# Attention and gated convolution: key sums moved between step 3's row work and `x`, groups of the last batch turned by DMA alone, and another order behind the last scores

## The chip, the cores and the metric

The kernel runs on one core of a Trainium2 chip. The metric is device time in microseconds (us). The measured kernel took 1134.94 us, the median of three runs that lay between 1133.9 and 1135.04 us. The engines are named as the profile names them: PE (TensorE matmuls), PEld (its weight loads), DVE (VectorE), ACT (ScalarE), POOL (GpSimd) and SP (SyncE, which here only issues DMAs). Each engine works off its own instructions strictly in program order.

## The reference, cut to what matters

```python
def _attn_ref(q, kv, w_sr):                 # q (4, 12288, 128), kv (4, 384, 32, 128)
    kv_pool = kv.reshape(B, H // r, r, W // r, r, C).mean(axis=(2, 4))     # r = 4
    k = v = kv_pool.reshape(B, -1, C) @ w_sr                               # 768 keys
    s = scale * (q @ k.transpose(0, 2, 1))
    a = np.exp(s - s.max(-1, keepdims=True))
    a /= a.sum(-1, keepdims=True) + 1e-09
    return a @ v

def _moe_ref(x, w_val, conv_w, w_out):      # x is the attention's output
    gate_pre[:, t] = sum(conv_w[k] * x[:, t - 4 + k] for k in range(5))    # causal, 5 taps
    return (sigmoid(gate_pre) * (x @ w_val)) @ w_out
```

All of it is float32. The last three weights reach the kernel as float64 words and are converted on the chip.

## The kernel before, in words

Channels lie on the partitions. There are 4 batches of 12288 queries and 768 keys. Queries are worked on in **groups** of 512, 24 to a batch, 96 in all; a group is four tiles of 128 queries, and the main loop (L470) makes one **step** for each tile, 384 steps, `gi` being the group and `j` (0 to 3) the step in it. The work of a step is written out by hand, and it belongs to several groups at once: scores are made one step ahead, and the groups that are 1, 2, 3 and 4 behind (`last`, `avg`, `xg`, `mg`) are in later stages.

What one tile goes through: three float32 products on PE give 128 x 768 scores `s` in PSUM (`score`, L250); DVE takes the negated row maximum `nm` (L256); ACT takes the exponential and its row sums `z` (L268). Each value is then split in two float16 halves, the high one by ACT (`p_hi`, L315), the low one by DVE one step later (`p_lo`, L319). The product with the values needs keys on the partitions, so tiles have to be turned. For tiles 0 to 2 (`NX = 3`), the halves go to a tile `hl` in SBUF, and a DMA transpose issued by SP writes them to `pt` (L323): one for tiles 0 and 1, issued behind the low half of tile 1, and one for tile 2, behind that of tile 2. Tile 3 is turned on PE instead (`turn`, L298): ACT writes the exponential to `pf`, six PE transposes of 128 x 128 put it back over the scores in PSUM, and the halves are written straight to `pt` (`pt<-s` in the profile).

Two groups later PE multiplies `pt` by the values, 18 products of 512 columns (`av`, L332), spread over the four steps as 7, 2, 3 and 6. Meanwhile DVE takes reciprocals of the row sums (`z`, L275, step 0), PE turns them (L278), DVE copies them out (`r`, L285, step 1), SP stores them (`rd`, L286) and reads them back to all partitions (`rb`, L291, step 3). In step 3 of the group that is two behind, DVE makes `x = av * down * rb` (L349), behind a 4-column copy by POOL (L345).

The second half of the network follows on `x`: taps and their sums on POOL (L359, L368; the fifth tap on ACT, L357), tanh on ACT (`th`, L384), the value product on PE in step 1 (`g_val`, L388, to `m`), `h` on DVE (L393), the output product on PE in step 2 (L398), a copy out on ACT (L408) and stores by SP in pairs of groups (L412). `m` is one PSUM bank, which the turned row sums, both products and the key setup use in turn.

Queries come in pairs of groups (L221) and are split in two on ACT (`qh`, L232) and POOL (`ql`, L236).

**Key setup.** A batch's keys come in 16 pieces of 384 KB (`load_kv`, L118, tile `kvt` with `AHEAD = 5` buffers). DVE sums each piece, 128 x 768 to 128 x 48 (`pool_kv`, L121), the whole is projected (L134), split (L143 to L147) and made into values. For batch 0 this is done ahead of the loop, and there every piece from the ninth on is followed by one operation of the weights' conversion (`convert`, 14 small DVE operations, L90 to L97); the other six are dripped in at two per step from step 6 on. For the next batch it is spread over the groups of the present one: `setup_steps` (L201) makes a list of which one entry is taken at the end of each group's step 3. An entry `piece(i)` issues the load of piece i + 2 (the first entry those of pieces 0, 1 and 2) and hands back the sum of piece i, which is executed in step 0 of the next group, behind `p_lo`. The entries for projecting and for the values follow. Small operations that a list `trickle` holds go out at two per step (`drip`).

```python
            return None, lambda: pool_kv(st, i)          # L208, executed at L513:
        if low and (j == 0 or t < NT):
            low()
```

Behind the loop (L536 on) the last groups, n1 (the last) to n5, are finished by a sequence written out by hand; there the gate of n2 and n1 is made on DVE (`conv_dve`, L374 and L376, tile `fast`), n1 in two halves of 256 columns.

## Time and profile before

| | us |
|---|---|
| median of the runs | 1134.94 |
| the profiled execution | 1133.22 |
| its span, first to last instruction | 1131.4 |
| PE busy | 1063.6 (94%) |
| DVE busy | 919.0 (81%) |
| ACT busy | 910.4 (80%) |
| POOL busy | 864.4 (76%) |
| key sums on DVE (L121), 64 of them | 60.5 |
| PE transposes of tile 3 (L298), 576 of them | 78.8 by modelled ends |
| time of the DMA packets of the SP queue, share of 16 engines | 85.4% |

The profile is of one execution. A busy share is a mean over the whole span. "Idle before" is the time an engine stood still ahead of an instruction, with what released it; the time at which one group follows another is read from an instruction that occurs once per group, here the reciprocal L275. Matmuls overlap and their ends are modelled, so on PE starts are compared, not durations. The mean granted clock of PE is 0.983 of full speed.

### The profile page before, as it was taken

The page shows a single profiled execution, that of the slowest core. Times are in us where ns is not written, and L with a number is a line of the kernel's source. Part 1 is how long each engine was busy: PE and PEld are TensorE (multiplying, and loading weights), DVE is VectorE, ACT ScalarE, POOL GpSimd, SP SyncE. Part 2 cuts the span into 40 slices and gives each one's busy share as a digit, 9 for nine tenths or more (in the row PEclk, how much of TensorE's full clock was granted, in tenths as well). Part 3 has the DMA queues.
Part 4 walks back from the last instruction along what each step waited for, and adds up shares of the span by engine and source line. Part 5 has one row for each costly group of instructions (what it writes and reads, how often), then busy time and mean ns, then how long its engine had stood idle before and what let it go on. Part 6 is the DMA issues. An engine that isn't in the chain of part 4 may idle for free.

```text
span 1131.4 us, 16595 instructions
## 1 busy us (share of the span) xinstructions
PE 1063.6 (94%) x5174; PEld 715.6 (63%) x5174; DVE 919.0 (81%) x1290; ACT 910.4 (80%) x1659; POOL 864.4 (76%) x948
## 2 busy tenths in 40 slices
PE   2879999999979999999997999999999999999996
PEld 1656666666756666666764666666666666666663
DVE  6868888888858888888885888888888888888884
ACT  1868888888858888888885888888888888888881
POOL 1168788878858888888885888887888888888872
PEclk9989999999989999999998999999999999999998
DMA  7779999887879999888876999898788888888872
GB/s 271 145 178 200 211 210 232 192 178 191 187 169 198 202 224 214 206 177 191 187 165 170 209 217 226 200 221 183 171 171 197 187 170 202 186 170 199 175 148 93
DMA packets 487095, 215.53 MB, mean 190 GB/s; under 512 B 453088, under 2 KB 453856, under 8 KB 487008
## 3 DMA queue, kind: packets, MB, share of 16 engines
q1 hardware_dynamic: 487008, 214.48, 85.4%
q8 instruction: 41, 0.67, 0.2%
q14 instruction: 46, 0.38, 0.1%
HBM read 75.83 MB, written 25.36 MB: 89 GB/s over the span
## 4 chain that ended last, share of the span: by engine, by line
PE 49%; DVE 25%; ACT 11%; issue 6%; POOL 5%; DMA 3%; SPq 1%; DVEq 0%; ACTq 0%
PE s L250 17%; PE av L332 16%; PE m L388 8%; DVE nm L256 8%; POOL ql L236 5%; ACT s L268 5%; DVE pool L121 4%; DVE pt L319 4%; ACT hl L315 4%; DVE x L349 4%; PE m L398 3%; PE s L298 3%; DMA kvt<-in_kv 3%; ACT qh L232 2%; DVE h L393 2%
## 5 line engine op out<-in xcount | busy, mean ns | idle before, releaser
L368 POOL TENSOR_TENSOR sum<-sum,tap 128x512 f32<-128x512 f32 x282 | 359.6, 1275 | 39.7 <-ACT tap L357 17.8
L332 PE MATMUL av<-pt,vh 128*128 128x512 f16 x1140 | 389.1, 383 | 0.0
L256 DVE TENSOR_REDUCE nm<-s 128x1 f32<-128x768 f32 x384 | 364.4, 949 | 3.7 <-PE s L250 3.7
L268 ACT ACTIVATE s<-s,nm 128x768 f32<-128x768 f32 x288 | 251.9, 875 | 125.5 <-DVE nm L256 124.3
L359 POOL TENSOR_SCALAR tap<-x,wm 128x512 f32<-128x512 f32 x376 | 253.4, 693 | 82.4 <-DVE x L349 80.9
L319 DVE SCALAR_TENSOR_TENSOR hl<-s,hl 128x768 f16<-128x768 f32 x288 | 273.1, 948 | 21.0 <-ACT hl L315 20.3
L250 PE MATMUL s<-kh,qh 128*128 128x384 f32 x768 | 253.3, 411 | 10.8 <-DVE hl L319 8.1
L315 ACT ACTIVATE hl<-s 128x768 f16<-128x768 f32 x288 | 233.3, 810 | 9.1
L332 PEld LDWEIGHTS <-vh 128*128 128x128 f16 x1164 | 114.0, 98 | 175.5 <-issue 85.8
L332 PE MATMUL av<-pt,vl 128*128 128x512 f16 x570 | 217.5, 382 | 0.0
L236 POOL TENSOR_TENSOR ql<-q,qh 128x512 fp32r<-128x512 f32 x96 | 121.8, 1269 | 122.6 <-ACT qh L232 122.6
L250 PE MATMUL s<-kh,ql 128*128 128x384 f32 x768 | 199.1, 341 | 0.0
L250 PE MATMUL s<-kl,qh 128*128 128x384 f32 x768 | 198.9, 340 | 0.0
L250 PEld LDWEIGHTS s<-kh,qh 128*128 128x128 f32 x768 | 132.4, 193 | 51.8 <-DVE hl L319 8.4
L349 DVE SCALAR_TENSOR_TENSOR x<-av,down,rb 128x512 f32<-128x512 f32 x95 | 71.4, 751 | 89.6 <-POOL ql L236 71.5
L250 PEld LDWEIGHTS s<-kl,qh 128*128 128x128 f32 x768 | 141.3, 190 | 0.5 <-DVE kl L147 0.5
L250 PEld LDWEIGHTS s<-kh,ql 128*128 128x128 f32 x768 | 140.9, 190 | 0.0
L388 PE MATMUL m<-x,wm 128*128 128x512 f32 x188 | 103.0, 630 | 25.0 <-DVE r L285 24.9
L368 POOL TENSOR_TENSOR sum<-tap,tap 128x512 f32<-128x512 f32 x94 | 120.4, 1281 | 0.0
L393 DVE SCALAR_TENSOR_TENSOR h<-th,m 128x512 f32<-128x512 f32 x94 | 64.7, 689 | 59.2 <-PE m L388 57.7
L315 ACT ACTIVATE pt<-s 128x768 f16<-128x768 f32 x96 | 77.8, 810 | 37.8 <-PE s L298 37.8
L332 PEld LDWEIGHTS <-vl 128*128 128x128 f16 x582 | 57.6, 99 | 77.9 <-issue 55.2
(68 smaller groups left out, 1068.9 us busy)
## 6 DMA issues: line engine op xcount, KB each, us to landing
kvt<-in_kv SPq DMA_DIRECT2D x64, 384.0 KB
rb<-rd SPq DMA_DIRECT2D x96, 256.0 KB
q<-in_q SPq DMA_DIRECT2D x47, 512.0 KB
out<-o SPq DMA_DIRECT2D x46, 512.0 KB
pt<-hl SPq DMA_TRANSPOSE x192
rd<-r SPq DMA_DIRECT2D x96, 2.0 KB
out<-o SPq DMA_DIRECT2D x3, 256.0 KB
q<-in_q SPq DMA_DIRECT2D x2, 256.0 KB
```

The source lines that it names most:

```text
L236: nc.gpsimd.tensor_tensor(out=g.ql, in0=g.q, in1=g.qh.bitcast(F32), op=ALU.subtract)
L250: nc.tensor.matmul(s[:, h, :HALF], a[:, sl], k[:, h * HALF:(h + 1) * HALF], start=(i == 0), stop=(i == 2))
L256: nc.vector.tensor_reduce(out=nm, in_=g.s[j], axis=AX.XY, op=ALU.max, negate=True)
L268: nc.scalar.activation(out=halves(g.pf[j]) if on_pe(j) else g.s[j], in_=g.s[j], func=AF.Exp, bias=g.nm.pop(j), accum_out=g.z[:, j:j + 1])
L315: nc.scalar.activation(out=part(g, j, 0), in_=g.s[j], func=AF.Copy, scale=2.0 ** 15)
L319: nc.vector.scalar_tensor_tensor(out=part(g, j, 1), in0=g.s.pop(j), scalar=2.0 ** 15, in1=part(g, j, 0), op0=ALU.mult, op1=ALU.subtract)
L332: nc.tensor.matmul(out, g.st[v][:, k * P:(k + 1) * P], g.pt[:, j0:j1, a * NCH + k], start=(i == 0), stop=(i == len(AV_ORDER) - 1))
L349: nc.vector.scalar_tensor_tensor(out=g.x[:, HALO + c0:HALO + c1], in0=av, scalar=g.st["down"], in1=g.rb[:, c0:c1], op0=ALU.mult, op1=ALU.mult)
L359: eng.tensor_scalar(out=g.tap[k], in0=src, scalar1=w, scalar2=1.0, op0=ALU.mult, op1=ALU.mult)
L368: nc.gpsimd.tensor_tensor(out=s, in0=acc, in1=g.tap[k], op=ALU.add)
L388: nc.tensor.matmul(m, wval, g.x[:, HALO + c0:HALO + c1], start=True, stop=True)
L393: nc.vector.scalar_tensor_tensor(out=h, in0=th, scalar=1.0, in1=m, op0=ALU.add, op1=ALU.mult)
```

## The change

- `NX` is replaced by a number of each group, `by_dma`: 4 for groups 0, 2, 4 ... 22 of the last batch, 3 for all others. With 4, no tile of the group is turned on PE: tile 3's halves go to `hl` (whose buffers grow from three tiles to four for all groups), and the DMA transposes are one for tiles 0 and 1 and one for tiles 2 and 3, the latter behind the low half of tile 3, so in step 0 of the next group.
- The sum of a piece is no longer handed back. The next entry of the list queues it in `pooling`, and it is executed in step 3 of the group after that, between `p_lo` and `x`. The list gets one entry more.
- The conversion of the weights leaves the prologue. All 14 operations go into `trickle` at step 3.
- The calls behind the loop are put in another order, with n1's two halves apart.

The diff:

```diff
@@ -17,7 +17,6 @@
 P = 128
 GQ = 512
 NT = GQ // P
-NX = 3
 
 
 class Group:
@@ -192,6 +191,7 @@
         return high, low
 
     trickle = []
+    pooling = []
 
     def value_steps(st):
         return [lambda: trickle.extend(column_scale(st)), lambda: None, lambda: None,
@@ -202,12 +202,13 @@
         def piece(i):
             if i == 0:
                 key_tiles(st)
+            else:
+                pooling.append(lambda: pool_kv(st, i - 1))
             for k in range(3) if i == 0 else (i + 2,):
                 if k < PIECES:
                     load_kv(b, st, k)
-            return None, lambda: pool_kv(st, i)
-
-        steps = [lambda i=i: piece(i) for i in range(PIECES)]
+
+        steps = [lambda i=i: piece(i) for i in range(PIECES + 1)]
         steps += [lambda h=h: project(st, h, misc()) or split_keys(st, h) for h in range(2)]
         return steps + value_steps(st)
 
@@ -256,16 +257,16 @@
         nc.vector.tensor_reduce(out=nm, in_=g.s[j], axis=AX.XY, op=ALU.max, negate=True)
         g.nm[j] = nm
 
-    def on_pe(j):
-
-        return j >= NX
+    def on_pe(g, j):
+
+        return j >= g.by_dma
 
     def expo(g, j):
         if j == 0:
             g.z = zs[g.i % len(zs)]
-        if on_pe(j):
+        if on_pe(g, j):
             g.pf[j] = pfp.tile([P, NK], F32, name="pf")
-        nc.scalar.activation(out=halves(g.pf[j]) if on_pe(j) else g.s[j], in_=g.s[j],
+        nc.scalar.activation(out=halves(g.pf[j]) if on_pe(g, j) else g.s[j], in_=g.s[j],
                              func=AF.Exp, bias=g.nm.pop(j), accum_out=g.z[:, j:j + 1])
 
     def norm_eps(g):
@@ -305,10 +306,10 @@
 
     def part(g, j, a):
 
-        if on_pe(j):
+        if on_pe(g, j):
             return pt_tile(g)[:, j, a * NCH:(a + 1) * NCH].rearrange("p (h k) q -> p h (k q)", h=2)
         if g.hl is None:
-            g.hl = hlp.tile([P, NX, 2, NK], F16, name="hl")
+            g.hl = hlp.tile([P, NT, 2, NK], F16, name="hl")
         return halves(g.hl[:, j, a])
 
     def p_hi(g, j):
@@ -318,8 +319,8 @@
 
         nc.vector.scalar_tensor_tensor(out=part(g, j, 1), in0=g.s.pop(j), scalar=2.0 ** 15,
                                        in1=part(g, j, 0), op0=ALU.mult, op1=ALU.subtract)
-        if j in (1, 2):
-            j0 = 0 if j == 1 else j
+        if (j % 2 or j == g.by_dma - 1) and not on_pe(g, j):
+            j0 = j // 2 * 2
             nc.sync.dma_start_transpose(
                 out=pt_tile(g)[:, j0:j + 1].rearrange("p j k q -> p (j k) q"),
                 in_=g.hl[:, j0:j + 1].rearrange("p j a k -> p (j a k)"))
@@ -421,6 +422,7 @@
         for i in range(NG):
             g = Group()
             g.i, g.b, g.t0, g.st = len(groups), b, i * GQ, states[b]
+            g.by_dma = 4 if b == B - 1 and i % 2 == 0 else 3
             g.s, g.nm, g.pf, g.hl, g.pt = {}, {}, {}, None, None
             groups.append(g)
     G = len(groups)
@@ -444,8 +446,6 @@
         if i == 3:
             convert = load_moe()
         pool_kv(st, i)
-        if i >= 8 and convert:
-            convert.pop(0)()
         if i == 3 * PIECES // 4:
             low()
         if i % (PIECES // 2) == PIECES // 2 - 1:
@@ -475,7 +475,7 @@
             load_pair(at(gi + 4), at(gi + 5))
         if gi % NG == 1 and j == 0 and at(gi + NG - 1):
             steps += setup_steps(cur.b + 1, states[cur.b + 1])
-        if t == NT + 2:
+        if t == 3:
             trickle += convert
 
         if nxt:
@@ -492,8 +492,9 @@
             high = None
         row_max(cur, j)
         expo(cur, j)
-        if on_pe(j):
+        if on_pe(cur, j):
             turn(cur, j)
+        if j == NT - 1:
             norm_eps(cur)
             if mg:
                 out_tile(mg)
@@ -513,6 +514,8 @@
         if low and (j == 0 or t < NT):
             low()
             low = None
+        if pooling and j == NT - 1:
+            pooling.pop(0)()
         if last and j == 0:
             norm_turn(last, misc())
         drip()
@@ -541,51 +544,51 @@
         return bank_pair()[:, 0]
 
     norm_reciprocal(n1)
-    p_lo(n1, NT - 1)
-    store_pair(n5)
+    av_part(n2, 0)
     norm_turn(n1, misc())
     n4.th = g_tanh(n4.gate)
-    norm_store(n1)
-    n4.m = g_val(n4, misc())
-    av_part(n2, 0)
-    norm_rows(n1)
     tap(n3, TAPS - 1, nc.scalar)
     g_conv(n3)
-    h = g_h(n4.th, n4.m)
+    p_lo(n1, NT - 1)
+    norm_store(n1)
+    store_pair(n5)
     for i in (1, 2, 3):
         av_part(n2, i)
+    norm_rows(n1)
+    n4.m = g_val(n4, misc())
     new_x(n2, n3, nc.scalar.copy)
     g_x(n2, n2.av)
-    n4.m = g_out(h, misc())
+    h4 = g_h(n4.th, n4.m)
     n2.m = g_val(n2, bank())
+    n4.m = g_out(h4, misc())
     out_tile(n4)
     g_evac(n4, n4.m)
     store(n4)
+    avs = [bank()[:, :half] for _ in cuts]
+    for i, av in enumerate(avs):
+        av_range(n1, av, 0, len(AV_ORDER), i * NT // 2, (i + 1) * NT // 2)
     n2.th = g_tanh(conv_dve(n2))
     new_x(n1, n2, nc.scalar.copy)
-    avs = [bank()[:, :half] for _ in cuts]
-    av_range(n1, avs[0], 0, len(AV_ORDER), 0, NT // 2)
-    h = g_h(n2.th, n2.m)
-    av_range(n1, avs[1], 0, len(AV_ORDER), NT // 2, NT)
+    g_x(n1, avs[0], *cuts[0])
+    h2 = g_h(n2.th, n2.m)
+    n2.m = g_out(h2, bank())
+    n1.th = work.tile([C, GQ], F32, name="th")
+    ths = [g_tanh(conv_dve(n1, *cuts[0]), n1.th[:, :half])]
     n3.m = g_val(n3, misc())
-    n2.m = g_out(h, bank())
-    ths = []
-    n1.th = work.tile([C, GQ], F32, name="th")
-    for av, c in zip(avs, cuts):
-        g_x(n1, av, *c)
-        ths.append(g_tanh(conv_dve(n1, *c), n1.th[:, c[0]:c[1]]))
+    n3.th = g_tanh(n3.gate)
     out_tile(n2)
     g_evac(n2, n2.m)
     store(n2)
-    n3.th = g_tanh(n3.gate)
-    h = g_h(n3.th, n3.m)
-    ms = [g_val(n1, bank()[:, :half], *c) for c in cuts]
-    hs = [g_h(th, m) for th, m in zip(ths, ms)]
-    n3.m = g_out(h, misc())
+    g_x(n1, avs[1], *cuts[1])
+    h3 = g_h(n3.th, n3.m)
+    ms = [g_val(n1, bank()[:, :half], *cuts[0])]
+    n3.m = g_out(h3, misc())
+    ths.append(g_tanh(conv_dve(n1, *cuts[1]), n1.th[:, half:]))
     g_evac(n3, n3.m)
     store(n3)
-    for h, c in zip(hs, cuts):
-        g_evac(n1, g_out(h, bank()[:, :half]), *c)
+    ms.append(g_val(n1, bank()[:, :half], *cuts[1]))
+    for th, m, c in zip(ths, ms, cuts):
+        g_evac(n1, g_out(g_h(th, m), bank()[:, :half]), *c)
         store(n1, *c)
```

## The prediction

> **What bounds the kernel now.** I read the page's busy shares first (PE 94%, so waits are few and local), then the reciprocal L275, which occurs once per group, by windows, for the pace of each stage. Columns: window, its length, DVE busy with these instructions (count), granted PE clock, DMA share, GB/s.
>
> ```profile
> 57.70:75.05 17.35, 0.17 (x1) 0.80 0.71 167
> 75.05:241.30 166.25, 2.51 (x15) 1.00 0.94 208
> 319.05:339.15 20.10, 0.17 (x1) 0.83 0.82 195
> ...
> 593.77:614.91 21.14, 0.17 (x1) 0.76 0.79 193
> 614.91:781.17 166.26, 2.51 (x15) 1.00 0.92 204
> 890.75:997.10 106.35, 1.68 (x10) 1.00 0.86 186
> ```
>
> Three paces stand there. Groups that sum keys take 166.25/15 = 11.08 us, 45 of them (the middle batch's 15 are the line left out). Groups of the last batch, which sum none, take 106.35/10 = 10.63. And one group in each of the first three batches takes 17.35, 20.10 or 21.14, at a lowered clock.
>
> What sets the two steady paces: the chain of waits in a key group (start, length, what), then DVE's and PE's timelines in a last-batch group (start, length, engine and line, in brackets the idle before).
>
> ```profile
> 419.47 0.28 DVE r L285
> 419.75 0.04 issue
> 419.79 1.14 PE m L388 x2
> ```
>
> ```profile
> 974.39 0.75 DVE L349 SCALAR_TENSOR_TENSOR x<-av,down,rb 128x512 f32<-128x512 f32 x1 [0.87 <-POOL ql L236]
> ...
> 977.72 0.27 DVE L285 COPY r<-m 4x128 f32<-4x128 f32 x1
> ...
> 985.00 0.75 DVE L349 SCALAR_TENSOR_TENSOR x<-av,down,rb 128x512 f32<-128x512 f32 x1 [0.87 <-POOL ql L236]
> ```
>
> ```profile
> 973.91 0.38 PE L332 MATMUL av<-pt,vh 128*128 128x512 f16 x1
> ...
> 978.53 1.02 PE L388 MATMUL m<-x,wm 128*128 128x512 f32 x2
> ...
> 989.15 1.02 PE L388 MATMUL m<-x,wm 128*128 128x512 f32 x2
> ```
>
> PE's value product (L388) writes the bank that `r` is copied from, so it can't start before `r` has ended. In the key group it starts 0.04 behind `r`: PE waits there, and a ring is closed, of x, row maximum, low half, key sum, row maximum, `r` (all DVE), value product and PE's work up to the last `av`, which the next x needs. In the last-batch group `r` ends at 977.99 and the product starts at 978.53, so the ring has 0.5 of slack and PE alone sets 989.15 - 978.53 = 10.62. The ring without a key sum is: product to x, 985.00 - 978.53 = 6.47 (x is released by the last `av`, which ends at 973.91 + 0.38 = 974.29, x starting at 974.39; the bracket's `ql` ends at the same time); x to the end of `r`, 977.99 - 974.39 = 3.60; and 0.04. Together 10.11. With a sum of 0.87 (row below) it is 10.98, and 11.08 was measured; 0.1 I can't place.
>
> The long groups have another cause, on DVE:
>
> ```profile
> 64.92 0.95 DVE L121 TENSOR_REDUCE pool<-kvt 128x48 f32<-128x768 f32 x1 [6.07 <-DMA kvt<-in_kv]
> ```
>
> The first piece's sum stands in DVE's queue one step after its load's issue; the row work behind it, and then PE, wait 6 us.
>
> **The change part by part.**
>
> *First sums.* A first sum now comes in step 3 of the second group behind its load, some 20 us after the issue, where the wait shown was 6.07. The wait goes, and what is late next is PE's own 10.62: 17.35 + 20.10 + 21.14 - 3 x 10.62 = **26.7**. The three loads issued together still put 1.1 MB ahead of the transposes and `rb`; I take nothing for it, and at most 1.5 in each of three groups.
>
> *The other sums.* In step 3 DVE stands idle 0.87 ahead of x (rows 974.39 and 985.00), and a sum takes 0.87 from start to start (row 22.58 below). It fits with nothing to spare, but even a later x doesn't count until the ring's 10.11 has grown by 0.5. So it costs nothing there and leaves the ring: 45 x (11.08 - 10.62) = **20.7**. If the cover were gone, each group would pay 0.87 less 0.5, some 17 of the 20.7. A buffer is free one group before the next load that takes it, so SP isn't held.
>
> Beside x there is a neighbour that step 0 didn't have, POOL's `ql`. Whether a sum on DVE is held by it, the prologue shows:
>
> ```profile
> 10.48 1.26 POOL L236 TENSOR_TENSOR ql<-q,qh 128x512 fp32r<-128x512 f32 x1 [9.18 <-ACT qh L232]
> ```
>
> ```profile
> 10.92 3.88 DVE L121 TENSOR_REDUCE pool<-kvt 128x48 f32<-128x768 f32 x4 [0.87 <-DMA kvt<-in_kv]
> ```
>
> Four sums, 0.97 each, start in the middle of a `ql` that ends at 11.74; neither is longer than elsewhere. I take nothing for it; a full hold is a rival below. The Trainium skill, page "SBUF — State Buffer", section "Who interferes with whom", has a rule that speaks against such neighbours: DVE and GpSimd share a port pair as an exclusive lock, and the loser blocks for the other's whole instruction. The same section exempts `tensor_reduce` on trn2, and the trace agrees: 0.97 beside a `ql`. By the lock alone the sum would come out as in that rival.
>
> *Last batch, even groups.* Their six PE transposes go, by the chain:
>
> ```profile
> 974.29 0.66 PE s L298 x6
> ```
>
> PE then needs 10.62 - 0.66 = 9.96, but the ring needs 10.11, and both meet at the value product, where PE waits in order and can't save up the rest. Saved: 0.51 x 12 = **6.1**; between 0 (something else sets these groups) and 12 x 0.66 = 7.9. ACT and DVE do the same work at other addresses. On SP's queue:
>
> ```profile
> 971.55 5.14 SPq L323 DMA_TRANSPOSE pt<-hl  x2
> ```
>
> Three tiles take 5.14, so two about 3.4. The second transpose now waits for the low half of tile 3, which DVE ends one row maximum ahead of `r`, near 976.9. It stands behind this step's `rb` and ahead of a store and of `rd`: issue to 980.3, `rd` about 2 later than now, which no one needs before the `rb` behind the next transposes; those come at 971.55 + 10.6 = 982.2. An estimate for its landing from the same row: 976.9 + 3.4 and half as much again, 982. The `av` that needs it begins about 1 behind the x of 985.00. Four microseconds are left, at a DMA share of 0.86 that rises by a third of the transposes in every second group.
>
> *Conversion.* The prologue's chain, and SP's issues of the last seven loads:
>
> ```profile
> 10.07 5.41 DMA kvt<-in_kv
> ...
> 16.46 0.20 DVE rest L90
> ...
> 22.58 0.87 DVE pool L121
> ```
>
> ```profile
> 10.07 7.80 SPq L118 DMA_DIRECT2D kvt<-in_kv  x7
> ```
>
> Seven conversions of 0.20 or somewhat more lie between the last sums; without them DVE could be done about 1.6 earlier. But the last load is issued near 17.5, and one took 5.41 to land, which is 22.9: the last sum (22.58) can hardly start earlier. I take **0.1**, between 0 and 1.6. In steps 4 and 5, where the pipeline fills and DVE is on the path, four operations of 0.20 come in; steps 6 to 8 had theirs before. I take **-0.6**, between 0 and -1.5.
>
> *Behind the last scores.* DVE's and ACT's rows, SP's `rb` for n2, and what an `rb` took to land in the chain:
>
> ```profile
> 1110.58 0.75 DVE L349 SCALAR_TENSOR_TENSOR x<-av,down,rb 128x512 f32<-128x512 f32 x1 [4.88 <-PE av L332]
> 1111.44 0.49 DVE L374 TENSOR_SCALAR fast<-x,wm 128x512 f32<-128x512 f32 x1
> 1111.96 3.11 DVE L376 SCALAR_TENSOR_TENSOR fast<-x,wm,fast 128x512 f32<-128x512 f32 x4
> ...
> 1117.35 2.05 DVE L376 SCALAR_TENSOR_TENSOR fast<-x,wm,fast 128x256 f32<-128x256 f32 x4
> ```
>
> ```profile
> 1128.33 0.38 ACT L408 ACTIVATE o<-s 128x256 f32<-128x256 f32 x1 [0.49 <-PE s L398]
> ```
>
> ```profile
> 1104.17 0.83 SPq L291 DMA_DIRECT2D rb<-rd  x1
> ```
>
> ```profile
> 74.83 2.89 DMA rb<-rd
> ```
>
> Now n2's `av` waits for a value product that waits for n1's `r`. Put first, its 18 products, for which DVE now waits 4.88, are done by about 1106. But n2's `rb`, issued at 1104.17 behind n1's transposes, lands 2.9 to 4 later, so x starts near 1108 instead of 1110.58. From there DVE sets the end: x 0.7, h of n4 0.6, gate 0.5 + 3.1, tanh 0.7, h 0.6, half a gate 2.4, half an x 0.5, h of n3 0.6, half a gate 2.4, tanh 0.5, half an h 0.4, half a product on PE about 1, copy 0.4: 14.4, to 1122.4, where it was 1128.71. That is 6.3. PE will idle for x once more, and a lowered clock (0.76 to 0.83 in the windows of the long groups) would hold up its 36 half products for n1. I take **5.0**, between 2 and 8.
>
> Sum: 26.7 + 20.7 + 6.1 + 0.1 - 0.6 + 5.0 = 58.0. The profiled execution took 1133.22, 1.8 more than its span of 1131.4 (the table above), and would take 1075.2; the median of the runs lies 1.72 above it: 1134.94 - 58.0 = **1076.9**.
>
> **The rivals.**
>
> *DMA takes over in the key groups.* For it: 0.94 at 11.08 is 10.4 of packet time a group, 0.98 at 10.62, and transposes and `rb` share one queue. Against it: in the whole span PE waited for a transpose 0.2 us:
>
> ```profile
> L332 PEld LDWEIGHTS <-vh 128*128 128x128 f16 x1164 | 114.0, 98 | 175.5 <-issue 85.8 <-DMA pt<-hl 0.2
> ```
>
> If these groups stay at 11.08, 20.7 is lost: 1097.6; half of that gives 1087.
>
> *The sum is held by `ql`.* Then it starts when `ql` ends, x slips by 0.87, the ring takes 10.98, and key groups stay at 11.0: 1094 to 1098. For it speaks the bracket at x, against it only the prologue's rows, in other surroundings.
>
> *The even groups give nothing.* The ring's unplaced 0.1 may be larger there, or ACT's work too tight: 1083.
>
> *Slower than before: the even groups' second transpose lands late.* It decides where it lands over 4 us later than I estimate. PE then stands at `av` in order, with all scores behind it. Groups in which the engines waited 6 us cost 6.7 to 10.5 each (windows above), clock included; twelve at 8.6 make 103, less the 51.9 of the other parts: 1186. It takes a two-tile transpose of over 8 us, where three tiles are issued in 5.14. The Trainium skill, page "TensorE: Matmul & The Clock Gate", Part 1, says that an idle window of about 3.4 us halves PE's clock; the windows' 0.76 to 0.83 agree.
>
> **How the numbers follow.** Forecast 0.80, DMA 0.07, `ql` 0.04, even groups nothing 0.07, late transpose 0.02. The low end takes all of 7.9, 8 behind the last scores and 1.6 in the prologue: 1076.9 - 6.3, rounded to 1070. The high end takes 2 behind the last scores (+3), the bursts (+4.5), and half of the DMA rival (+10): 1094. Outside are the full rivals near 1097 and the late transpose, 0.13 at most. About 0.2% is what a measurement of this kernel can tell from no change. Only the late transpose ends above it: faster 0.97, slower 0.02, and 0.01 for parts that cancel.
>
> **What would show it.** L275 should follow itself at 10.62 in key groups; in the loop no L121 should wait for its load and no interval exceed 12 us; in the last batch intervals near 10.1 and 10.6 should take turns. n2's x should start 17 to 18 before the span's end. The forecast is wrong if key groups stay above 10.8, if x starts more than 0.2 behind the last `av`, or if PE waits for `pt`.

## The result and the profile after

The changed kernel takes 1077.99 us, median of runs from 1075.04 to 1078.68; the kernel before, measured beside it, 1134.42 (1132.55 to 1135.04). The ratio is 0.950, 95% interval 0.9478 to 0.9522. The forecast was 1076.9. The profiled execution took 1078.68 with a span of 1076.9, which is 54.5 less than the span before; all of the following is about these 54.5.

First the reciprocal, now L276, by windows for the same stages as before (window, length, DVE busy with it, granted clock, DMA share, GB/s):

```profile
59.88:68.93 9.05, 0.17 (x2) 1.00 1.00 235
68.93:228.47 159.54, 2.50 (x15) 1.00 1.00 220
305.50:316.82 11.32, 0.17 (x1) 1.00 0.94 221
...
563.93:575.26 11.33, 0.17 (x2) 1.00 0.96 220
575.26:734.43 159.17, 2.50 (x16) 1.00 1.00 223
810.76:1051.02 240.26, 3.84 (x24) 1.00 0.98 202
1051.02:1076.91 25.89, 0.16 (x1) 0.91 0.42 116
```

Groups that sum keys follow each other at 159.54/15 = 10.64, 159.17/15 = 10.61 (11.08 before). The three long groups are 9.05, 11.32 and 11.33, at full clock (17.27, 20.09 and 21.13 before, from reciprocal to reciprocal; the prediction's windows read up to 0.08 more). The DMA share has risen from 0.94 to 1.00, and between the third and the last reciprocal neither PE nor DVE waits for a transfer. Where the 54.5 came from, as differences of these intervals between the two profiled executions:

| part | forecast | measured |
|---|---|---|
| first sums (three long groups, and the values groups that move into them) | 26.7 | 28.2 |
| the other 45 sums | 20.7 | 20.6 |
| last batch, even groups | 6.1 | 3.7 |
| up to the third reciprocal (conversion) | -0.5 | -2.1 |
| behind the last reciprocal | 5.0 | 4.1 |
| sum | 58.0 | 54.5 |

The setup list is one entry longer, so one 11.3 us group that makes values moves from the stretch ahead into the place of each long group; that is why two of these read 11.32 and not 10.62, and 0.70 has gone from each of the stretches ahead. The first row counts both. Likewise two such groups now stand at the start of the last batch: as a stretch it takes 240.26 against 242.48, and the third row has the 1.4 that moved into it taken out.

The key sum beside x, in DVE's and POOL's timelines of a key group:

```profile
408.98 0.96 DVE L320 SCALAR_TENSOR_TENSOR hl<-s,hl 128x768 f16<-128x768 f32 x1 [0.23 <-ACT hl L316]
409.86 0.94 DVE L120 TENSOR_REDUCE pool<-kvt 128x48 f32<-128x768 f32 x1
410.81 0.75 DVE L350 SCALAR_TENSOR_TENSOR x<-av,down,rb 128x512 f32<-128x512 f32 x1
```

```profile
409.54 1.27 POOL L237 TENSOR_TENSOR ql<-q,qh 128x512 fp32r<-128x512 f32 x1 [0.40 <-ACT qh L233]
```

The sum fills exactly the 0.87 in which DVE stood idle, and runs its usual 0.94 wholly beside `ql` (409.54 to 410.81); so do all 48 sums of the loop. The chain of waits in such a group consists of PE alone:

```profile
327.50 1.53 PE av L333 x7
329.03 0.11 PE m L279
329.14 1.07 PE s L251 x6
330.21 0.86 PE m L389 x2
```

No work of another engine stands in it. Over the whole span the profile's page gives this chain by engine, where before it gave PE 49% and DVE 25%:

```profile
PE 89%; DVE 5%; ACT 2%; DMA 2%; issue 1%; POOL 0%; SPq 0%; DVEq 0%; ACTq 0%
```

From 40 us on none of the 48 sums found DVE waiting for a load.

### The profile page after: what moved, and what is told of

It is laid out like the page before. It is cut to its first block, busy times and chain, and to the rows that moved or that the text cites. A ratio compares the mean times of both kernels' runs of the same rounds, so it can differ in the third digit from the quotient of the medians.

```text
span 1076.9 us, 16475 instructions
## 1 busy us (share of the span) xinstructions
PE 1038.4 (96%) x5102; PEld 706.5 (66%) x5102; DVE 919.5 (85%) x1290; ACT 903.7 (84%) x1659; POOL 865.2 (80%) x948
## 4 chain that ended last, share of the span: by engine, by line
PE 89%; DVE 5%; ACT 2%; DMA 2%; issue 1%; POOL 0%; SPq 0%; DVEq 0%; ACTq 0%
PE s L251 36%; PE av L333 32%; PE m L389 7%; PE m L399 7%; PE s L299 5%; DMA kvt<-in_kv 2%; DVE nm L257 1%; PE m L279 1%; ACT s L269 1%; ACT hl L316 1%; DVE hl L320 1%; DVE pt L320 1%; DVE pool L120 0%; DVE x L350 0%; PE m L176 0%
## 5 line engine op out<-in xcount | busy, mean ns | idle before, releaser
L369 POOL TENSOR_TENSOR sum<-sum,tap 128x512 f32<-128x512 f32 x282 | 360.3, 1278 | 22.1
L269 ACT ACTIVATE s<-s,nm 128x768 f32<-128x768 f32 x300 | 262.0, 873 | 88.7 <-DVE nm L257 80.0
L320 DVE SCALAR_TENSOR_TENSOR hl<-s,hl 128x768 f16<-128x768 f32 x300 | 284.8, 949 | 21.4 <-ACT hl L316 21.1
L316 ACT ACTIVATE hl<-s 128x768 f16<-128x768 f32 x300 | 243.0, 810 | 9.1
L399 PE MATMUL m<-h,wm 128*128 128x512 f32 x188 | 96.8, 597 | 1.2 <-DVE h L394 1.2
L389 PE MATMUL m<-x,wm 128*128 128x512 f32 x188 | 96.1, 592 | 0.0
```

Of the source, the lines that this page charges most:

```text
L269: nc.scalar.activation(out=halves(g.pf[j]) if on_pe(g, j) else g.s[j], in_=g.s[j], func=AF.Exp, bias=g.nm.pop(j), accum_out=g.z[:, j:j + 1])
L316: nc.scalar.activation(out=part(g, j, 0), in_=g.s[j], func=AF.Copy, scale=2.0 ** 15)
L320: nc.vector.scalar_tensor_tensor(out=part(g, j, 1), in0=g.s.pop(j), scalar=2.0 ** 15, in1=part(g, j, 0), op0=ALU.mult, op1=ALU.subtract)
L369: nc.gpsimd.tensor_tensor(out=s, in0=acc, in1=g.tap[k], op=ALU.add)
L389: nc.tensor.matmul(m, wval, g.x[:, HALO + c0:HALO + c1], start=True, stop=True)
L399: nc.tensor.matmul(m, wout, h, start=True, stop=True)
```

## The experiments

### The key sums: which step, how late, how much more

`late_step0` keeps the sum two groups behind its load but puts it back in step 0; `x_first` keeps step 3 but puts it behind x.

```diff
-        if pooling and j == NT - 1:
+        if pooling and j == 0:               # late_step0
```
```diff
-        if pooling and j == NT - 1:          # x_first: these two lines
-            pooling.pop(0)()                 # go behind new_x and g_x
```

> The changed kernel with the late sums put back into step 0 (one group later than in the kernel before, behind the low half of tile 3). Theory, the ring: a sum that lies between x and the copy of r is part of the ring x, r, value product, last av. The waits for the first loads stay away, but key groups go back from 10.62 to 11.08 us each: 48 x 0.46 = 22 us more than the changed kernel, about 1099. Rival, lateness: what helped the 45 other groups too was that the sum no longer comes close behind its load; then step 0 is as good as step 3 and the time stays near 1078.

> The changed kernel with the sum in the same step 3, but behind x instead of ahead of it. Theory, the ring: the sum now lies between x and r, so key groups take about 11.0 to 11.1 again, 1097 to 1100, although step, load and neighbours are the same. Rival, the balance of steps: the gain came from taking the sum out of step 0, where DVE has the reciprocal and the low half as well; then the order within step 3 makes no difference and the time stays near 1078.

Measured: 1100.12 (ratio 0.9704, 0.9687 to 0.972) and 1100.14 (0.9704, 0.9687 to 0.9722). By windows of the reciprocal in `late_step0`:

```profile
311.69:323.01 11.32, 0.17 (x1) 1.00 0.93 221
323.01:488.87 165.86, 2.51 (x15) 1.00 0.97 214
```

And in its chain, the ring is back, `r` and then the product:

```profile
402.76 0.28 DVE r L286
...
403.09 1.14 PE m L389 x2
```

The long groups are cured in both kernels (11.32), so it is the lateness that removes 26.7 or more; the key groups are at 165.86/15 = 11.06 in one and 166.55/15 = 11.10 in the other, so it is the place ahead of x that gives the 20.7. One instruction further, behind x, the sum is in a ring again and the whole gain of this part is gone. So the two gains can be told apart. In `x_first` it is not `r` that PE waits for: its products start 0.16 behind `r` and not 0.05, and the scores ahead of them 0.06 behind the end of tile 3's low half. That second way is taken up below, with the even groups.

`early_step3` lets each entry queue its own piece, so that the sum comes one group behind its load, ahead of x:

```diff
-            else:
-                pooling.append(lambda: pool_kv(st, i - 1))
             ...
+            pooling.append(lambda: pool_kv(st, i))
-        steps = [lambda i=i: piece(i) for i in range(PIECES + 1)]
+        steps = [lambda i=i: piece(i) for i in range(PIECES)]
```

> The changed kernel with the sum in step 3 beside x, but one group behind its load instead of two (an entry of the list queues the sum of its own piece). Theory, the ring: key groups stay at 10.62; the first sum of a batch comes one period (10.6 us) after the issue of three loads, which took about 9 us to land in the kernel before, so it waits between 0 and 2 us in three groups: 1078 to 1084. Rival, lateness: the 20 us of the key groups came from the later sum, and are given back: about 1098.

Measured: 1077.21 (0.9506, 0.9487 to 0.9525), equal to the changed kernel; by windows:

```profile
305.74:316.35 10.61, 0.17 (x1) 1.00 1.03 268
316.35:475.55 159.20, 2.51 (x15) 1.00 0.99 219
```

In the loop one sum of 48 waited for its load, 0.2 us, and one x waited 0.9 for its `rb` (an interval of 11.48, followed by 10.23). So step 3 of the next group is late enough, or nearly: the medians don't tell the two apart. The "about 9 us" of the expectation was too much; in the kernel before, the three loads land within 7.2 to 8.0 us of the first one's issue.

`extra_full` puts a second sum of the same size, whose output nothing uses, ahead of each real one in step 3:

```diff
-                pooling.append(lambda: pool_kv(st, i - 1))
+                pooling.append(lambda: more(st, i - 1) or pool_kv(st, i - 1))
```

> The changed kernel with each sum of the loop made twice (the first time into a tile that nobody reads), both ahead of x in step 3. Theory, the ring: the idle time ahead of x (0.87) holds one sum; a second one moves x by 0.87, of which the ring has 0.5 to spare in a group that PE sets at 10.62, by the r way, or 0.3 if the score bank's way (10.29 in the even groups of the last batch) is the longer one. So key groups take 11.0 to 11.2 and the time is 1095 to 1104. Rival, DVE is not near a limit there and x is not on a ring: the second sum goes into other idle time of DVE (h waits 0.8 for PE in each group) and the time stays below 1083.

Measured: 1092.98 (0.9645, 0.9625 to 0.9665). The key groups take 10.98 (window), and x now starts behind the second sum (DVE's timeline):

```profile
321.26:486.01 164.75, 2.52 (x15) 1.00 0.98 216
```

```profile
406.75 0.94 DVE L127 TENSOR_REDUCE pool<-kvt 128x48 f32<-128x768 f32 x1
407.61 0.74 DVE L357 SCALAR_TENSOR_TENSOR x<-av,down,rb 128x512 f32<-128x512 f32 x1
```

So the first sum is free and the second costs 0.36 of its 0.87: the rest is slack between x and PE. The size is that of the prediction's slack of 0.5, and the time, 1092.98, lies below my 1095 to 1104. But the slack that is used up is not the one over `r`. PE in the same group:

```profile
409.91 0.27 PE L286 MATMUL m<-ident,z 128*128 128x128 f32 x1
410.20 0.61 PE L258 MATMUL s<-kh,qh 128*128 128x384 f32 x2
```

The scores start 0.29 behind the turned row sums (0.03 in the changed kernel's key groups) and 0.06 behind the end of tile 3's low half, and the value product 0.16 behind `r`: as in `x_first`, PE waits for the low half here.

`only_sums` is the kernel before with nothing but the sums moved as in the change.

> The kernel before with the first part of the change alone: the sums two groups behind their loads and in step 3 ahead of x. Theory: it brings 26.7 for the first sums and 20.7 for the others, so 47.4 less than before, about 1086.5. Rival, the parts need each other (for instance the prologue's conversion or the longer list): a sum further than 3 us from that.

Measured: 1084.02 (0.9565, 0.9552 to 0.9578), 49.5 below the 1133.52 of the kernel before on the same chip. By windows:

```profile
58.00:67.04 9.04, 0.17 (x2) 1.00 1.08 224
...
314.93:474.13 159.20, 2.51 (x16) 1.00 1.02 223
...
1052.52:1081.98 29.46, 0.17 (x1) 0.88 0.39 102
```

The sums alone are nine tenths of the change. The 2 us above the 47.4 of the forecast lie mostly in the third interval, which falls to 9.04 and not to 10.62. A window count of the value product in the changed kernel says why:

```profile
59.88:68.93 9.05, 0.00 (x0) 0.00 (x0) 1.00 1.00 235
68.93:79.50 10.57, 1.02 (x2) 0.36 (x2) 1.00 1.08 249
```

The pipeline isn't full yet: this group has not the two value products (the count of 0 in the first row), and the same count gives no output products either; each pair is 0.86 in the chain, and 10.62 - 2 x 0.86 = 8.90. I had taken the steady pace for a group that doesn't run at it.

### The last batch: what the even groups' ring is

`no_even` turns every group's tile 3 on PE again.

```diff
-            g.by_dma = 4 if b == B - 1 and i % 2 == 0 else 3
+            g.by_dma = 3
```

> The changed kernel with tile 3 turned on PE in all groups (by_dma 3 everywhere). Theory, the ring: in the changed kernel the groups without PE transposes take 10.29 us against 10.61, so this kernel is 11 or 12 x 0.32 = 3.7 us slower than the changed one, about 1081.5. The forecast on record had 6.1 for it (10.11 a group). Rival, the even groups give nothing in the end, since DMA is fuller and the tail pays it back: no difference.

Measured: 1079.97 (0.9531, 0.9514 to 0.9548). The last batch's 23 intervals take

```profile
808.94:1053.14 244.20, 3.85 (x23) 1.00 0.85 179
```

where the changed kernel takes 240.26: 3.9 for the even groups, not 6.1. (The medians are 2.0 apart and the intervals of the two ratios overlap; the 3.9 is read from the two profiles.) The changed kernel's even groups are at 10.29 and its odd ones at 10.60, so the direction is right and the floor is 10.29, not 10.11. And only eleven of the twelve get shorter: the first lies where values are made and takes 11.31, against 11.33 in `no_even`. DVE and PE of the changed kernel in an even group show which wait makes the 10.29:

```profile
894.52 0.75 DVE L350 SCALAR_TENSOR_TENSOR x<-av,down,rb 128x512 f32<-128x512 f32 x1 [0.87 <-POOL ql L237]
...
896.14 0.93 DVE L320 SCALAR_TENSOR_TENSOR hl<-s,hl 128x768 f16<-128x768 f32 x1
...
897.85 0.27 DVE L286 COPY r<-m 4x128 f32<-4x128 f32 x1
...
904.81 0.75 DVE L350 SCALAR_TENSOR_TENSOR x<-av,down,rb 128x512 f32<-128x512 f32 x1 [0.87 <-POOL ql L237]
```

```profile
896.85 0.27 PE L279 MATMUL m<-ident,z 128*128 128x128 f32 x1
897.21 0.59 PE L251 MATMUL s<-kh,qh 128*128 128x384 f32 x2
...
898.34 1.02 PE L389 MATMUL m<-x,wm 128*128 128x512 f32 x2
899.20 0.38 PE L333 MATMUL av<-pt,vl 128*128 128x512 f16 x1
```

The low half of tile 3 (896.14) is the last reader of that tile's scores. It ends at 897.07, and the scores that PE makes next, into the banks that come free, start at 897.21 instead of following the turned row sums directly as in odd groups (0.03 behind them). From there six matmuls take 1.13 and the value product follows. So there is a second ring, x, row maximum, low half, scores, value product: 898.34 - 894.52 = 3.82, and product to x 6.47 as forecast, together 10.29. `r` ends at 898.12, 0.2 earlier than PE needs it. Two experiments were to test that.

`low_first` puts the low half ahead of the row maximum behind even groups, to hand the banks back 0.9 earlier.

```diff
+        early = j == 0 and prev and prev.by_dma == 4
+        if early:
+            p_lo(prev, NT - 1)
         row_max(cur, j)
         expo(cur, j)
...
-        if prev:
+        if prev and not early:
```

> The changed kernel with one swap in step 0 behind a group without PE transposes: the low half of tile 3 ahead of the row maximum. Theory: those groups take 10.29 and not 10.11 because the third bank pair of scores comes free only when this low half has ended (x, row maximum, low half, scores for step 2, value product, last av); the swap takes 0.87 out of that way, the way over r stays at 10.11, so the intervals become 10.11 and the time falls by 11 x 0.18 = 2 us, to about 1076. Rival, ACT: its exponential then waits 0.8 longer for the row maximum, and ACT becomes late; the intervals become 10.4 or more and the time rises by 1 to 4 us.

Measured: 1086.39 (0.9582, 0.9569 to 0.9596), 8.4 slower than the changed kernel where I had expected 2 faster. Its intervals are 11.84 and 9.88 by turns, 21.72 for two groups where the changed kernel takes 20.89. ACT's and PE's timelines:

```profile
919.98 0.88 ACT L269 ACTIVATE s<-s,nm 128x768 f32<-128x768 f32 x1 [1.95 <-DVE z L276]
```

```profile
920.12 0.30 PE L279 MATMUL m<-ident,z 128*128 128x128 f32 x1 [0.56 <-DVE z L276]
920.17 0.59 PE L251 MATMUL s<-kh,qh 128*128 128x384 f32 x2
```

The scores follow the turned sums after 0.05, but that says nothing of the banks: the swap puts the reciprocal behind the low half too, so the turned sums themselves start 3.05 behind x, where the scores started 2.69 behind it. The row maximum is now late for the exponential (ACT idle for 1.95, against 0.74 in the changed kernel), which is the rival's way, at more than its 1 to 4 us. So this run is no test of the second ring; it shows only that this order of DVE's work can't be had for nothing.

`delay_two` adds a short reduction of 0.3 in step 0 behind even groups, in the first six of them ahead of the low half, in the others behind it. If only the way over the low half counts, the first costs 0.3 and the second what is left after `r`'s slack.

```diff
+        extra = j == 0 and prev and prev.by_dma == 4
+        if extra and gi % NG < 12:
+            delay()
         if prev:
             p_lo(prev, (j - 1) % NT)
+        if extra and gi % NG >= 12:
+            delay()
```

> The changed kernel with one small DVE reduction more (128 x 256, about 0.3 us, into a tile that nobody reads) in step 0 behind each group without PE transposes: ahead of the low half of tile 3 in the first six such groups of the last batch, behind it in the other six. Theory, the score bank: the 10.29 us of these groups come by way of the low half, which frees the bank that step 2's scores wait for, and the way over r is shorter by about 0.18. So ahead of it the reduction costs its full length (intervals of 10.55 to 10.65), behind it 0.18 less (10.40 to 10.50). Rival, r (the way that the forecast on record priced at 10.11): both places lie ahead of r, so both cost the same. Second rival, PE or another engine sets 10.29: neither costs anything.

Measured: 1081.99 in a single run; even intervals 10.61 with the delay ahead, 10.55 with it behind (10.29 without). PE in a group of the first kind, then one of the second:

```profile
877.60 0.58 PE L255 MATMUL s<-kh,qh 128*128 128x384 f32 x2 [0.41 <-DVE hl L324]
...
984.52 1.12 PE L393 MATMUL m<-x,wm 128*128 128x512 f32 x2
985.48 0.38 PE L337 MATMUL av<-pt,vl 128*128 128x512 f16 x1
```

Ahead of the low half the delay counts in full, as it must on this ring. Behind it it counts 0.26, more than the 0.1 to 0.2 expected. The last two rows show why: a value product that had to wait for `r` is followed by the next instruction 0.96 later, one that didn't wait 0.86 later (898.34 and 899.20 above). Such a start costs 0.10. So `r`'s ring is 10.11 + 0.10 = 10.21, only 0.08 shorter than the other, and 10.21 + 0.33 = 10.54, against 10.55 measured. The same 0.10 is the "0.1 I can't place" of the prediction: in the kernel before, the product at 419.79 waits for `r` and its next instruction starts at 420.75, again 0.96 later; 10.98 + 0.10 = 11.08. In `late_step0` all 48 products that wait for `r` are followed 0.96 later, in the changed kernel none is. As `x_first` and `extra_full` show PE waiting for the low half too, the second ring doesn't rest on this single run.

`all_dma` has no tile turned on PE in any group of the last batch but the last.

```diff
-            g.by_dma = 4 if b == B - 1 and i % 2 == 0 else 3
+            g.by_dma = 4 if b == B - 1 and i < NG - 1 else 3
```

> The changed kernel with all groups of the last batch but the very last turned by DMA alone, instead of every second. Theory, the ring of 10.29 sets any group without PE transposes, and DMA has room: 11 more groups save 0.32 each, 3.5 us, about 1074.5, with all intervals at 10.29. Rival, DMA is the next limit: packet time per group rises to about 11.4 us at a share of 0.99 now, transposes and rb land later from group to group, PE waits for pt or DVE for rb, and the time is above the changed kernel's, by 0 to 15 us.

Measured: 1079.03 (0.9519, 0.9501 to 0.9536), no better than the change. By windows, and in the chain:

```profile
810.72:1049.29 238.57, 3.86 (x23) 1.00 1.04 220
```

```profile
961.40 6.63 DMA pt<-hl
...
968.17 1.67 PE av L333 x7
```

Most intervals are 10.28 to 10.30, the same floor, now in all groups. But at a DMA share of 1.04 transposes take long to land, this one 6.63 and the longest in the chain 7.55, PE waits for some, and single intervals read 10.49, 10.56, 10.61 and 11.22. The stretch gains 1.7, and the tail loses it again: its first x waits for an `rb` and starts 8.77 behind the last reciprocal, where the changed kernel's starts 6.99 behind it. The late transpose, my rival on the slow side, does exist, but only when more is turned by DMA than the change does, and at most 0.9 in a group.

### Conversion and tail

`convert_old` puts the conversion back: eight operations between the last sums of the prologue, six from step 6 on.

```diff
+        if i >= 8 and convert:
+            convert.pop(0)()
...
-        if t == 3:
+        if t == NT + 2:
```

> The changed kernel with the weights' conversion where it was (eight operations in the prologue, six from step 6 on). Theory: the prologue is set by its loads, so the first reciprocal comes within 0.3 us of the changed kernel's; the first two intervals fall from 21.9 to 20.1, of which the third gives back most (9.0 to 10.6), so the time is 0.2 to 0.8 us less, about 1077.5. Rival, the move shortens the prologue: then putting it back costs 1 to 1.6 us.

Measured: 1076.24 (0.9493, 0.948 to 0.9506). By windows:

```profile
37.41:57.92 20.51, 0.33 (x2) 1.00 0.94 172
```

Against the changed kernel the first reciprocal comes at 37.41 instead of 38.02 and the next two intervals take 20.51 instead of 21.86; the third stays at 9.05, so nothing is given back. The medians differ by 1.8, or by 1.2 if each is set against the kernel before beside it, and the intervals of the ratios overlap. The other profiles say how much of that is chance, since none of the other edits touches this stretch:

| | first reciprocal | next two intervals | third reciprocal |
|---|---|---|---|
| old conversion (before, `only_sums`, `convert_old`, `best`) | 37.4 to 37.7, mean 37.6 | 20.1 to 20.5, mean 20.3 | 57.7 to 58.0, mean 57.9 |
| new conversion (the change and nine others) | 36.1 to 38.0, mean 36.9 | 21.4 to 23.0, mean 22.1 | 57.9 to 60.1, mean 59.0 |

The prologue is 0.6 shorter on average, and the first groups take 1.8 more: a loss of 1.1, and everything else in the change has to pay for it. The changed kernel's own profile is 0.9 worse than this mean.

`tail_old` has the old order behind the last scores and all else of the change (its diff is the last part of the change's, reversed).

> The changed kernel with the calls behind the last scores in the order of the kernel before. Theory: the stretch behind the last reciprocal goes back from 24.4 to 25.9 us (24.4 where PE's clock is not halved within it) to about 29.5, so 4 us more, about 1082. Rival, most of the shorter tail comes from the last group's transposes and not from the order: below 1 us.

Measured: 1080.78 (0.9539, 0.9526 to 0.9552). By the medians that is 2.8 more than the changed kernel, where I had said 4 and the rival below 1; the intervals of the ratios just fail to overlap. Behind the last reciprocal it takes 28.08, where the changed kernel takes 25.89. But this stretch also varies between kernels that have the same order there: 24.4 and 24.5 in `no_even`, `early_step3` and `extra_full`, 25.6 to 25.9 in `late_step0`, `x_first`, `convert_old`, `low_first` and `delay_two`, 27.6 in `all_dma`. PE by windows of 2 us, first the changed kernel, then `no_even` (length, PE busy, granted clock, DMA share, GB/s):

```profile
1057.02:1059.02 2.00, 0.20 (x1) 0.95 0.67 257
1059.02:1061.02 2.00, 2.00 (x3) 0.50 0.26 65
1061.02:1063.02 2.00, 2.00 (x9) 0.70 0.00 0
```

```profile
1059.14:1061.14 2.00, 0.35 (x1) 1.00 0.68 257
1061.14:1063.14 2.00, 2.00 (x9) 1.00 0.17 51
```

PE stands idle until n2's x in both, which in `no_even` waits for `rb`; in the changed kernel the clock is then halved for 3.4 us, from 7.8 to 11.2 behind the last reciprocal, in `no_even` it isn't. The half products of n1 run in that window. DVE's x of n1 waits 1.63 for them in the changed kernel and not at all in `no_even`:

```profile
1064.54 0.48 DVE L350 SCALAR_TENSOR_TENSOR x<-s,down,rb 128x256 f32<-128x256 f32 x1 [1.63 <-PE s L333]
```

In all six kernels at 25.6 to 25.9, the change among them, a halved stretch of 3.4 us begins 7.7 to 9.0 behind the last reciprocal, in `all_dma` at 10.2; in the three at 24.4 and 24.5 none does before 22.9. (The 27.6 of `all_dma` is the late x told above.) The Trainium skill, page "TensorE: Matmul & The Clock Gate", Part 1, says that the clock looks at activity in windows of 3.4 us that run on by themselves, whatever the kernel does. The profiles agree: lengths of 3.41, places that differ.

Within each profile the halved stretches behind the last reciprocal start whole multiples of 3.41 apart, so its time can be divided into windows of 3.41. PE is idle for 2.3 to 2.7 us (by modelled ends) ahead of n2's value product in all nine kernels from 24.4 to 25.9. In the six with a halved stretch behind it, the window just ahead of that stretch holds 2.07 to 2.66 of this idle time; in the three without, no window holds more than 1.43, 1.71 and 1.79. So the same wait costs a halved clock or nothing by where the windows fall. (The kernel before has one halved stretch behind a window with 1.78, so where the line lies is not shown.)

The old order fared worse by its windows, too. All three profiles with it, 28.08, 29.46 and 29.95, have halved stretches (mean clocks 0.94, 0.88 and 0.83). In the kernel before, one lies from 3.5 to 6.9 behind the last reciprocal, while PE makes n2's `av`, and n2's x starts at 9.12. In `tail_old`, at full clock until 21.1, it starts at 7.44:

```profile
1058.20 0.75 DVE L350 SCALAR_TENSOR_TENSOR x<-av,down,rb 128x512 f32<-128x512 f32 x1 [3.20 <-PE av L333]
```

In the changed kernel it starts at 6.99. So putting n2's products first brings that x 0.45, and not the 2.6 of the prediction. In all, the order is worth 28.08 - 25.89 = 2.2 against the changed kernel, and 3.6 to 3.7 against the three kernels at 24.4 and 24.5.

### The better of each part

`best` takes `early_step3`, the conversion of `convert_old`, DMA turning in three groups of four of the last batch, and issues n1's half products earlier, ahead of n2's value product and n4's output product.

```diff
-            g.by_dma = 4 if b == B - 1 and i % 2 == 0 else 3
+            g.by_dma = 4 if b == B - 1 and i % 4 != 3 else 3
```

> Four edits to the changed kernel: the conversion back in the prologue, the sum one group behind its load, three of four groups of the last batch without PE transposes instead of two, and behind the last scores the two half products for n1 ahead of n2's value product, so that PE does not stand idle while DVE waits for rb. Theory: -1.5 for the conversion, 6 x 0.32 = -1.9 for the groups less what fuller DMA takes back (0 to 1), and a tail that stays at 24.4 or less because PE's clock is not halved: about 1074, between 1072 and 1076. Rival, the halved clock in the tail comes from elsewhere, or the half products come late for n2: then the tail is 25.5 to 27 and the sum of the edits gives nothing against the changed kernel's 1078.

Measured: 1074.70 (1074.59 to 1075.43; ratio 0.9486, 0.9473 to 0.9499), the lowest of all. It is 3.3 below the changed kernel's median; the kernel before was 0.9 quicker beside it, so some 2.4 are left, and the intervals of the two ratios overlap. The last batch:

```profile
811.26:1047.71 236.45, 3.85 (x23) 1.00 1.03 214
```

Three intervals of four are at 10.28 to 10.30 and the fourth is at 10.61; with that fourth group turned on PE, no interval of the last batch is longer, unlike in `all_dma`. Two things came otherwise than forecast. The tail takes 24.95 and not 24.4 or less: no stretch is halved before 22.8, but x of n2 waits for its `rb` and starts at 7.45. That the filled gap keeps the clock up isn't shown, since three kernels without it kept theirs. And with the conversion back, the sum one group behind its load does wait, 0.8 for the first load of the loop, and one x waits 1.1 for its `rb`.

## Why the prediction was right

*First sums: right, 1.5 too small.* The wait is gone, and `late_step0` shows that the lateness did it. The step "what is late next is PE's own 10.62" was mis-sized in the first batch, where a group needs only 9.05 (9.04 in `only_sums`). The up to 1.5 for the bursts that I kept in the range didn't come.

*The other sums: right.* 20.6 against 20.7, and for the reason given: `x_first` and `late_step0` lose all of it, `extra_full` shows that the cover is 0.87 long and hardly more. That the slack behind it came out at 0.5 is in part luck: it is the way over the low half that ends it, which the prediction didn't have. Of the rivals, DMA as the bound falls (10.61 at a share of 0.99 to 1.02), and the sum held by `ql` falls (0.94 beside it). On the latter the prediction's row said less than it was taken for: of its four sums only the first lay beside that `ql`, the second starts at 11.90.

*Even groups: the direction right, the way that sets them and the size wrong.* The term that was mis-sized is "the ring needs 10.11". I followed one way from x to the value product, over `r`, left out that a product that waits starts 0.10 more slowly, and didn't look at the banks that the scores need. That way is 10.21, the one over the low half 10.29; and eleven groups gain, not twelve: 11 x (10.61 - 10.29) = 3.5 in place of 6.1. The second transpose is in time, as forecast; SP's row:

```profile
897.09 3.63 SPq L324 DMA_TRANSPOSE pt<-hl  x1
```

It is issued until 900.72, for which I had 980.3 - 974.39 = 5.9 behind x; here it is 6.2. No `av` waited for a `pt` in the profile's waits.

*Conversion: mis-sized.* In the changed kernel's profile the last sum starts at 22.67 (22.50 in DVE's timeline before; the prediction's 22.58 is the chain's), waiting for its load, as the prediction had it; the 0.6 that the prologue gains on average is within the 0 to 1.6. The step that failed is the other one, four operations of 0.20 in steps 4 and 5: there are eight more than before in the first groups, and DVE has hardly a gap there, in whose timeline they take 0.20 to 0.52 from start to start. The prediction counted the four of steps 4 and 5 and overlooked that as many come in behind step 8. Not 0.6 but 1.8 is lost.

*Tail: the steps behind x right, the step ahead of it not.* n2's x starts 6.99 behind the last reciprocal, where "near 1108" meant 6.5; with the full clock of `no_even` x to the end of the last copy is 14.8, forecast 14.4, and x to the end of the span 17.6, forecast 17 to 18. In the changed kernel's profile the halved clock adds the rest, 18.9. I had named this and taken 5.0 of 6.3 for it; 4.1 was measured. That this is near is in part luck: I read the 4.88 that x waited in the kernel before as the price of the order, but `tail_old` shows that most of the 2.1 by which x now comes earlier (9.12 to 6.99) was the halved clock of that profile. The order alone is worth 2.2 to 3.7.

The profiles' 54.5 is 3.5 short of the 58.0, with errors of both signs in it. That the medians nevertheless lie 56.4 apart, and the profiled executions 54.5, is spread: the profiled one is the slowest of the changed kernel's runs, whose spans reach from 1073.3 at a mean clock of 1.000 to 1076.9 at 0.996. That the halved window in the tail makes this difference too is argued from the profiled kernels, not shown for those runs.

## What to carry to other kernels

An operation that must be done somewhere costs nothing where its engine waits for something that it can't hurry, and one instruction further its length less the ring's slack (here 0.49 of 0.87 in each group); so find the ring that sets the pace, and the one idle gap in it, before moving work. When a ring is shortened, walk every way between its two fixed points, over the buffers that have to come free as well as over the data: the second longest way is the new floor. Differences of 1 to 2 us behind the end of a loop may be the clock's phase and no merit of the order; compare the granted clock there first.

## What the runs showed of the hardware that I had not expected

A value product that had to wait for `r` was followed by the next instruction 0.96 later in place of 0.86, in the key groups of the kernel before as in the delayed groups of `delay_two`. The DMA share reads 0.99 to 1.03 over 160 to 236 us without one transfer being late for PE; only at 1.04 with still more transposes did PE wait, up to 1.1 at a time. A wait of PE of 2.3 to 2.7 us cost a halved clock for 3.41 us when 2.07 or more of it fell into one window of 3.41, and nothing when 1.79 or less did, in nine kernels with the same order there.
